# Attention's inner order on one core: one value run at the head of every key step, scores with the second head first, seven and nine products between the runs

## The chip, the cores and the metric

The kernel runs on one core of one Trainium2 chip. The metric is the device time of one execution in microseconds (us), smaller is better. Names of engines as in the profile: PE is TensorE (PEld its weight loads), DVE is VectorE, ACT is ScalarE, POOL is GpSimd, SP is SyncE with its DMA queue.

## The reference

One transformer block on x of shape (1, 2048, 576) with a conditioning vector c: attention with 32 heads of 18 features each, then a gated feed-forward part of width 4608.

```
mod = silu(c) @ w_mod                      # six rows of 576: sa, ca, ga, sb, cb, gb
h   = layernorm(x) * (1 + ca) + sa
q, k, v = heads(h @ wqkv)                  # 32 heads of 18
p   = softmax(q k^T * 18**-0.5)            # over all 2048 keys
x   = x + ga * (p v) @ wo
h   = layernorm(x) * (1 + cb) + sb
x   = x + gb * (sigmoid(h @ w_gate) * (h @ w_up)) @ w_down
```

## The kernel before, in words

The program has three stretches: layer norm and the q, k, v projections (0 to about 269 us of the profiled execution), attention (to about 1621 us), and the feed-forward part (to the end). The change is in attention.

Attention goes through 32 units. A unit is a pair of heads and one half (1024) of the queries; it takes 16 steps, `kt` = 0 to 15, one for each 128 keys. A step makes four score products, `t` in the order tables (line 955): for each head `h` of the pair and each chunk `c` of 512 queries, keys against queries into a 128x512 tile in PSUM (the on-chip memory for sums), which ACT takes through exp into a tile `p` in SBUF (line 959). Keys and queries of head 0 lie in partitions 0 to 55 and those of head 1 in partitions 64 to 119, so the two heads' products use different halves of PE's rows; each product names one half only.

For the softmax's maximum the kernel runs the products of the unit ahead a second time, queries against keys (`maxima`, line 442, `m` in the tables, one for each call of `turn`). They come in rounds of eight, and their head alternates, 0, 1, 0, 1. Of a round's eight, the first (head 0) is taken up by ACT (line 448, tile `rise`), the third (head 0) by DVE in a custom instruction that also reads `rise` (line 450), and the other six by a DVE maximum (line 455). In each pair of steps one round is done, beginning with its second product: in order the heads are 1, 0, 1, 0, 1, 0, 1, 0, and the last is the one for ACT.

Both kinds of product take their PSUM bank from one ring of seven: `bank()` hands out `s0` to `s6` in turn, so the eighth product waits until the first one's bank has been read by ACT or DVE. The transposes and projections below use the same ring.

`values()` (`v`, line 533) adds probabilities times values for one step, the one two steps back (`LAG`): four products in the program, eight instructions in the trace, each on 32 columns of PE and all 128 rows, into the one bank `o`. Called a value run here. A `w` in the table, once in two steps, is the place for all other work that goes between: `taken` and `outputs` (copy of `o` on ACT, line 547, and four transposes, line 557, once a unit), `spread` (one transpose, line 471, once a unit), and the steps of `rows0` and `rows1` in the second half of attention (transposes at lines 639, 656, 785 and the output projection, line 672, 14 or 9 products at a time).

PE's order is written by hand (`manual_schedule`): it does exactly what the tables say. The other engines' orders are set by a scheduler from the same program.

```
STEPS = "vtmmttmvtm", "tmttwmtmm"      # even kt, odd kt
c, h = divmod(len(probs), 2)           # scores: head 0 first
```

An even step has both value runs; an odd step has none. Read as one cycle, six products lie between the first run and the second (`t m m t t m`), and ten between the second and the next first (`t m t m t t w m t m m`).

Of the kernel before, what the change touches and what calls it, by code (L numbers as in the profile page):

```python
# [15 lines left out]
F32 = mybir.dt.float32  # L16
# [7 lines left out]
P = 128  # L24
# [19 lines left out]
NB = F // 256  # L44
LAG = 2

STEPS = "vtmmttmvtm", "tmttwmtmm"
ORDERED = 56


# [1 line left out]
def tile_block(ctx, tc, x_in, wqkv, wo, w_gate, w_up, w_down, c_in, w_mod, out):  # L52
# [25 lines left out]
    def bank():  # L78

        turns["bank"] += 1  # L80
        return ps.tile([P, 512], F32, name=f"s{turns['bank'] % 7}")


    def load_mod(a, b, i):

        cols = slice(2 * D * i, 2 * D * (i + 1))
        for t in range(0, 4, 2):
            rows = slice(t * P, (t + 2) * P)
            nc.sync.dma_start(a[:, t : t + 2, :], w_mod[rows, cols].rearrange("(t p) c -> p t c", p=P))
        nc.sync.dma_start(b[0:64, :], w_mod[DM:D, cols])  # L90
        return [a[:, t, :] for t in range(4)] + [b]
# [307 lines left out]
    def heads(u):  # L399
        return qsets[u % 3], ksets[u if u < 2 else 2 + (u - 2) % 3]  # L400

    def load_heads(u):


        qs, ks = heads(u)
        half, p = divmod(u, H // 2)
        own = slice(half * HW, (half + 1) * HW)
        for h in range(2):
            rows = slice((2 * p + h) * DH, (2 * p + h + 1) * DH)
            two, one = (slice(64 * h + a, 64 * h + b) for a, b in ((0, 2 * DH), (2 * DH, 3 * DH)))  # L410
            nc.sync.dma_start(
                qs[two, :].bitcast(F32), qd[:, rows, own].rearrange("l f n -> f l n").bitcast(F32)
            )
            nc.sync.dma_start(qs[one, :].bitcast(F32), qd[0, rows, own].bitcast(F32))
            wide = S if h or u < 2 else S + 512
            nc.sync.dma_start(
                ks[two, 0:wide].bitcast(F32),
                kd[0, rows, 0:wide].unsqueeze(1).to_broadcast([DH, 2, wide]).bitcast(F32),
            )
            nc.sync.dma_start(ks[one, 0:wide].bitcast(F32), kd[1, rows, 0:wide].bitcast(F32))  # L420
# [65 lines left out]
    def turn():  # L486
        if turns["s"] < turns["to"]:
            turns["s"] += 1
            next(todo, None)
# [26 lines left out]
    ppool = att.enter_context(tc.tile_pool(name="ppool", bufs=LAG + 1))  # L516
# [25 lines left out]
    def taken():  # L542

        if "whole" in state:
            half, p, acc = state.pop("whole")
            oT = epool.tile([P, 512], F32, name="oT")
            nc.scalar.copy(oT, acc)  # L547
            state["end"] = (half, p, oT)

    def outputs():  # L550

        if "end" not in state:
            return
        half, p, oT = state.pop("end")
        tp = bank().rearrange("p (b q) -> p b q", q=P)
        for b in range(4):
            nc.tensor.transpose(tp[:, b, :], oT[:, b * P : (b + 1) * P], ident)  # L557

        tq = tp.rearrange("p b (j e) -> p j b e", e=32)
        rec = epool.tile([P, 4, 4], F32, name="rec")  # L560
        nc.vector.reciprocal(rec, tq[:, :, :, DH])
        if half == 1 and p == H // 2 - 1:
            state["last"] = epool.tile([P, 512], F32, name="oT")[:, 0 : 16 * DH].rearrange("p (t e) -> p t e", t=8)
            for h in range(2):
                nc.vector.tensor_tensor(
                    state["last"][:, :, h * DH : (h + 1) * DH].rearrange("p (c b) e -> p c b e", c=2),
                    tq[:, 2 * h : 2 * h + 2, :, 0:DH],
                    rec[:, 2 * h : 2 * h + 2, :].unsqueeze(3).to_broadcast([P, 2, 4, DH]),
                    op=ALU.mult,
                )  # L570
            return
        nc.scalar.copy(oT, tp.rearrange("p b q -> p (b q)"))
        tq = oT.rearrange("p (b j e) -> p j b e", j=4, e=32)
        for h in range(2):
            f0 = (2 * p + h) * DH
            nc.gpsimd.tensor_tensor(
                Os[half][:, :, f0 : f0 + DH].rearrange("p (c b) e -> p c b e", c=2),
                tq[:, 2 * h : 2 * h + 2, :, 0:DH],
                rec[:, 2 * h : 2 * h + 2, :].unsqueeze(3).to_broadcast([P, 2, 4, DH]),
                op=ALU.mult,  # L580
            )
# [341 lines left out]
    for u in range(UNITS):  # L923
        half, p = divmod(u, H // 2)
        qs, ks = heads(u)
        if 0 < u < UNITS - 2:
            load_heads(u + 2)
        if u == H // 2:
            Os.append(big.tile([P, 8, 640], F32, name="big"))
        for kt in range(NT):  # L930
            step = u * NT + kt
            turns["to"] = 65 + 4 * LEAD + 4 * (step + 1)
            kcols = slice(kt * P, (kt + 1) * P)
            probs = []
            for does in STEPS[kt % 2]:
                if does == "m":
                    turn()
                elif does == "w":
                    if kt == 3:
                        outputs()  # L940
                    taken()
                    if "spread" in state:
                        spread(*state.pop("spread"))
                    if FROM0 <= step < FROM1:
                        next(rows0, None)
                    if step >= FROM1:
                        next(rows1, None)
                elif does == "v":
                    if step >= LAG:
                        values()  # L950
                else:
                    c, h = divmod(len(probs), 2)
                    sT = bank()
                    rows = slice(64 * h, 64 * h + 3 * DH + 2)
                    nc.tensor.matmul(  # L955
                        sT, ks[rows, kcols], qs[rows, c * 512 : (c + 1) * 512], start=True, stop=True
                    )
                    pr = ppool.tile([P, 512], F32, name=f"p{len(probs)}")
                    state["exp"] = nc.scalar.activation(pr, sT, AF.Exp, scale=SCALE)  # L959
                    probs.append(pr)  # L960
            pending.append((half, p, kt, probs))
            if u in (1, 3):
                if kt == 2:
                    a = big.tile([P, 8, 640], F32, name="big")
                    a = a.rearrange("p a b -> p (a b)")[:, 0 : 8 * D].rearrange("p (t c) -> p t c", t=4)
                    b = slots.tile([P, 2560], F32, name="w0")[:, 0 : 2 * D]
                    mods = load_mod(a, b, 1 + u // 2)
                    row = slots.tile([P, 2560], F32, name="w1")[:, 0:544]
                elif kt == 10 and u == 1:
                    modulate(row, mods, HALVES, [(None, None), (mcol2[:, 1, :], 0.0)])  # L970
                elif kt == 10:
                    modulate(row, mods, HALVES, [(mcol2[:, 0, :], 1.0), (gb_b, None)])
            if 4 * NT <= step < FROM0 and step % 2 == 0:
                next(downs, None)
            if step == FROM0:
                for _ in downs:
                    pass
            if step == FROM1 - 1:
                for _ in rows0:
                    pass  # L980
                bgs.close()
                raws = ctx.enter_context(tc.tile_pool(name="raws", bufs=1, side="right"))
            if u == 30 and kt == 7:
                first = [load_block(raws, 0, k, paced) for k in range(2)]
            if u >= 30 and kt == 2:
                load_x(u - 30, f"k{u - 30}")
            if u == UNITS - 1 and kt == 3:
                nc.sync.dma_start(oend[:, :, 0 : D - DL - 2 * DH], Os[1][:, :, DL : D - 2 * DH])
            if u == UNITS - 1 and kt == 9:
                for _ in rows1:  # L990
                    pass
                load_x(2, "w0")
                load_x(3, "w1")
                both = big.tile([P, 2, 5, 512], F32R, name="big")
                for i in range(2):
                    X[5 + i] = both[:, i]
                    load_x(5 + i)
                begun = {"b": 0, "half": 0, "raw": first}
                for k in ORDER[:2]:
                    weights_operand(begun, k, True)  # L1000
# [281 lines left out]
```

## Time and profile before

| | |
|---|---|
| time, median of 3 runs | 2952.17 us (2949.37 to 2953.37) |
| the profiled execution | 2953.87 us, span 2952.1 us, clock 0.993 |
| attention, about | 269 to 1621 us of the span, 256 pairs of steps |
| PE busy there | 1345.09 of 1352.00 us |
| ACT busy there | 1208.67 us |
| DVE busy there | 1143.04 us |

The span is the time from the first to the last instruction; 1.8 us of the profiled execution lie around it. The profiled execution is 1.7 us above the median of the runs. [...]

### The profile page before, as it was taken

To read this page: it belongs to the slowest core of one execution; us is meant where nothing else is said; L and a number is where in the kernel's file an instruction comes from. 1 tells how busy PE (TensorE), PEld (TensorE's weight loads), DVE (VectorE), ACT (ScalarE), POOL (GpSimd) and SP (SyncE) were. 2 spreads that over 40 slices of the span, in tenths; PEclk is the share of its full clock that TensorE was granted. 3 is DMA by queue.
4 is the path that set the end of the run, shared out by engine and by line. 5 is a ranking of instruction groups with operands and counts; after the bars stand their busy time and mean duration, and the time that the engine had idled before them with its cause. 6 is when DMAs were issued, how large, how long until landed. Compare 5 with 4: busy or idle time off the path is not lost.

```text
span 2952.1 us, 46641 instructions
## 1 busy us (share of the span) xinstructions
PE 2890.3 (98%) x17141; PEld 1888.9 (64%) x17141; DVE 2139.3 (72%) x3896; ACT 1614.7 (55%) x3022; POOL 813.7 (28%) x972
## 2 busy tenths in 40 slices
PE   7999999999999999999999999998999999999999
PEld 5756333433344444444443788877888888888888
DVE  7465888888888888998883777766777555555555
ACT  3214889999999888999889323333333111111111
POOL 3102005444303111464103534467544100000000
PEclk9999999999999999999999999999999999999999
DMA  5325213333302111222214766676666845444443
GB/s 178 101 87 185 71 31 131 121 130 126 117 26 80 53 33 44 90 75 70 60 62 161 271 237 235 232 265 237 217 215 217 317 161 178 166 166 170 162 157 136
DMA packets 137261, 425.97 MB, mean 144 GB/s; under 512 B 18884, under 2 KB 56520, under 8 KB 124744
## 3 DMA queue, kind: packets, MB, share of 16 engines
q1 hardware_dynamic: 121272, 342.42, 34.2%
q0 software_dynamic: 15760, 80.56, 7.6%
q8 instruction: 135, 2.21, 0.3%
q14 instruction: 94, 0.77, 0.1%
HBM read 264.45 MB, written 157.95 MB: 143 GB/s over the span
## 4 chain that ended last, share of the span: by engine, by line
PE 90%; ACT 2%; DVE 2%; DMA 2%; POOL 2%; issue 1%; SPq 1%; POOLq 0%; DVEq 0%; ACTq 0%
PE o L533 17%; PE d L1063 14%; PE x L1027 14%; PE s L955 13%; PE s L442 11%; PE bg L1027 5%; PE bu L1027 5%; PE s L294 4%; PE s L330 2%; PE s L672 2%; ACT p L959 1%; PE s L557 1%; ACT oT L547 1%; POOL S L875 0%; DMA B<-hs 0%
## 5 line engine op out<-in xcount | busy, mean ns | idle before, releaser
L959 ACT ACTIVATE p<-s 128x512 f32<-128x512 f32 x2048 | 1068.5, 608 | 142.9 <-PE s L442 91.7
L455 DVE TENSOR_REDUCE mx<-s 128x1 f32<-128x512 f32 x1568 | 1019.6, 686 | 169.7 <-PE s L442 156.2
L442 PE MATMUL s<-k,q 54*128 54x512 f32 x1920 | 649.7, 439 | 2.1 <-ACT p L959 1.6
L955 PE MATMUL s<-q,k 56*128 56x512 f32 x1920 | 578.7, 433 | 2.6
L955 PEld LDWEIGHTS s<-q,k 56*128 56x128 f32 x1920 | 274.8, 186 | 472.8 <-ACT p L959 304.7
L533 PE MATMUL o<-p,vaug 128*32 128x512 f32 x4096 | 555.8, 608 | 0.0
L1063 PE MATMUL d<-wd,hh 128*128 128x288 f32 x2304 | 470.0, 299 | 17.7 <-DVE Oa L1067 17.1
L1063 PEld LDWEIGHTS d<-wd,hh 128*128 128x128 f32 x2304 | 379.5, 191 | 26.9 <-DVE Oa L1067 21.5
L1067 DVE TENSOR_TENSOR Oa<-Oa,d 128x288 f32<-128x288 f32 x576 | 257.7, 452 | 152.6 <-PE d L1063 149.0
L442 PEld LDWEIGHTS s<-k,q 54*128 54x128 f32 x1920 | 308.4, 185 | 69.3 <-ACT p L959 38.5
L1063 PE MATMUL d<-wd,hl 128*128 128x288 f32 x1152 | 344.0, 299 | 0.0
L1027 PE MATMUL x<-k,w 128*128 128x512 f32 x994 | 239.6, 392 | 2.2 <-DVE u L1241 2.2
L1039 ACT ACTIVATE u<-u 128x512 f32<-128x512 f32 x72 | 45.5, 632 | 328.4 <-DVE u L1229 309.7
L1063 PEld LDWEIGHTS d<-wd,hl 128*128 128x128 f32 x1152 | 219.9, 191 | 0.3 <-DVE hl L1043 0.3
L1027 PEld LDWEIGHTS x<-k,w 128*128 128x128 f32 x994 | 184.7, 188 | 39.6 <-DVE u L1241 2.9
L533 PEld LDWEIGHTS o<-p,vaug 128*32 128x32 f32 x4096 | 83.5, 108 | 164.9 <-issue 149.4
L1069 POOL DMA_DIRECT2D out_dram<-Oa x16 | 8.7, 542 | 607.5 <-DVE Oa L1067 607.5
L1036 ACT ACTIVATE sg<-x 128x512 f32<-128x512 f32 x36 | 21.5, 598 | 282.5 <-PE x L1027 282.5
L450 DVE CUSTOM_DVE_ANT_0 rise<-s,rise 128x512 f32<-128x512 f32 x240 | 163.5, 681 | 0.0
L448 ACT ACTIVATE rise<-s 128x512 f32<-128x512 f32 x240 | 151.4, 631 | 0.0
L914 POOL TENSOR_TENSOR w<-S,w 64x256 fp32r<-64x256 f32 x69 | 72.0, 1044 | 214.2 <-ACT w L909 202.5
L1027 PE MATMUL x<-w,w 128*128 128x512 f32 x504 | 121.3, 390 | 0.0
(240 smaller groups left out, 3812.8 us busy)
## 6 DMA issues: line engine op xcount, KB each, us to landing
w<-ws SPq DMA_DIRECT2D x126, 640.0 KB
ws<-w SPq DMA_DIRECT2D x124, 640.0 KB
wd<-wds SPq DMA_DIRECT2D x36, 1152.0 KB
wds<-w POOLq DMA_DIRECT2D x18, 1152.0 KB, 4.5
k<-kd SPq DMA_DIRECT2D x30, 360.0 KB
w<-in_B_w_down_dram POOLq DMA_DIRECT2D x18, 576.0 KB, 5.0
q<-qd SPq DMA_DIRECT2D x64, 144.0 KB
raw<-in_B_w_gate_dram SPq DMA_DIRECT2D x34, 256.0 KB
```

Source lines behind the costliest of these rows:

```text
L294: nc.tensor.matmul(acc, w, hT[:, t, cols], start=n == 0, stop=n == len(ts_) - 1)
L442: nc.tensor.matmul(sp, qs[rows, qt * P : (qt + 1) * P], ks[rows, kc * 512 : (kc + 1) * 512], start=True, stop=True,)
L448: nc.scalar.activation(rise, sp, AF.Relu)
L450: nc.vector.tensor_tensor_reduce(rise, sp, rise, 1.0, -3.0e38, ALU.add, ALU.max, mx[0][:, qt, 0:1])
L455: nc.vector.tensor_reduce(mx[h][:, qt, j : j + 1], sp, axis=AX.X, op=ALU.max)
L533: nc.tensor.matmul(acc[32 * j : 32 * j + 32, :], vaug[:, kt, (2 * p + h) * VW : (2 * p + h) * VW + 32], probs[2 * c + h], start=kt == 0, s ...
L914: eng.tensor_sub(w[rows, :, to, :], src[rows, :, a, :], w[rows, :, a, :].bitcast(F32))
L955: nc.tensor.matmul(sT, ks[rows, kcols], qs[rows, c * 512 : (c + 1) * 512], start=True, stop=True)
L959: state["exp"] = nc.scalar.activation(pr, sT, AF.Exp, scale=SCALE)
L1027: nc.tensor.matmul(acc[v], w[:, v, a, :], X[s][:, b, :], start=first and n == 0, stop=n == 6, skip_group_check=not first,)
L1063: nc.tensor.matmul(acc[:, :HALF], a[:, f, rows], w[:, f, cols], start=n == 0, stop=n == 5)
L1067: nc.vector.tensor_add(Oa[:, t, cols], Oa[:, t, cols], acc[:, :HALF])
```

## The change

Two edits in the loop over steps. The tables put one value run at the head of each step instead of two in the even step, and move one maximum product from the even step to the odd one. And the scores of a step are taken with head 1 first for each chunk; the tiles keep their names, so `values` reads the same ones in the same order.

```
-STEPS = "vtmmttmvtm", "tmttwmtmm"
+STEPS = "vtmmtmtt", "vmtmttwmtmm"
...
-            probs = []
+            probs, at = [None] * 4, 0
...
-                    c, h = divmod(len(probs), 2)
+                    c, h = at // 2, 1 - at % 2
+                    at += 1
...
-                    pr = ppool.tile([P, 512], F32, name=f"p{len(probs)}")
+                    pr = probs[2 * c + h] = ppool.tile([P, 512], F32, name=f"p{2 * c + h}")
...
-                    probs.append(pr)
```

Read as one cycle, seven products now lie between the first run and the second (`t m m t m t t`) and nine between the second and the next first (`m t m t t w m t m m`). The score product moves from line 955 to 956 and its exp from 959 to 960.

PE in an even step, from the first value run's end through the second run, and one product more. L955 (956) is a score, L442 a maximum product, L533 a value product; the tile behind the operation is the bank. Before:

```order
L955 MATMUL s1_14742<-q0_981,k1_2184 128x512
L442 MATMUL s2_14746<-k2_2187,q1_982 128x512
L442 MATMUL s3_14749<-k2_2187,q1_982 128x512
L955 MATMUL s4_14752<-q0_981,k1_2184 128x512
L955 MATMUL s5_14756<-q0_981,k1_2184 128x512
L442 MATMUL s6_14760<-k2_2187,q1_982 128x512
L533 MATMUL o_14737<-p0_14704,vaug_97 32x512
L533 MATMUL o_14737<-p2_14715,vaug_97 32x512
L533 MATMUL o_14737<-p1_14711,vaug_97 32x512
L533 MATMUL o_14737<-p3_14728,vaug_97 32x512
L955 MATMUL s0_14767<-q0_981,k1_2184 128x512
```

The same place now:

```order
L956 MATMUL s1_14742<-q0_981,k1_2184 128x512
L442 MATMUL s2_14746<-k2_2187,q1_982 128x512
L442 MATMUL s3_14749<-k2_2187,q1_982 128x512
L956 MATMUL s4_14752<-q0_981,k1_2184 128x512
L442 MATMUL s5_14756<-k2_2187,q1_982 128x512
L956 MATMUL s6_14759<-q0_981,k1_2184 128x512
L956 MATMUL s0_14763<-q0_981,k1_2184 128x512
L533 MATMUL o_14737<-p0_14711,vaug_97 32x512
L533 MATMUL o_14737<-p2_14728,vaug_97 32x512
L533 MATMUL o_14737<-p1_14704,vaug_97 32x512
L533 MATMUL o_14737<-p3_14715,vaug_97 32x512
L442 MATMUL s1_14771<-k2_2187,q1_982 128x512
```

A score has come ahead of the second value run, and the run is followed by a maximum product instead of a score.

PE behind the second run, in the pair of steps where the four transposes of a unit's output stand at `w`, before:

```order
L955 MATMUL s0_14767<-q0_981,k1_2184 128x512
L442 MATMUL s1_14771<-k2_2187,q1_982 128x512
L955 MATMUL s2_14774<-q0_981,k1_2184 128x512
L442 MATMUL s3_14778<-k2_2187,q1_982 128x512
L955 MATMUL s4_14781<-q0_981,k1_2184 128x512
L955 MATMUL s5_14785<-q0_981,k1_2184 128x512
L557 MATMUL s6_14789<-ident_66,oT_14717 128x128 x4
L442 MATMUL s0_14803<-k2_2187,q1_982 128x512
L955 MATMUL s1_14806<-q0_981,k1_2184 128x512
L442 MATMUL s2_14810<-k2_2187,q1_982 128x512
L442 MATMUL s3_14813<-k2_2187,q1_982 128x512
```

And now:

```order
L442 MATMUL s1_14771<-k2_2187,q1_982 128x512
L956 MATMUL s2_14774<-q0_981,k1_2184 128x512
L442 MATMUL s3_14778<-k2_2187,q1_982 128x512
L956 MATMUL s4_14781<-q0_981,k1_2184 128x512
L956 MATMUL s5_14785<-q0_981,k1_2184 128x512
L557 MATMUL s6_14789<-ident_66,oT_14717 128x128 x4
L442 MATMUL s0_14803<-k2_2187,q1_982 128x512
L956 MATMUL s1_14806<-q0_981,k1_2184 128x512
L442 MATMUL s2_14810<-k2_2187,q1_982 128x512
L442 MATMUL s3_14813<-k2_2187,q1_982 128x512
```

Five products instead of six stand ahead of the other work, and the same four behind it; what differs in these four is the score's head.

ACT's exps of the same even step, in order, before (p0 and p2 are head 0, p1 and p3 head 1):

```order
L959 ACTIVATE p0_14744<-s1_14742 128x512
L959 ACTIVATE p1_14754<-s4_14752 128x512
L959 ACTIVATE p2_14758<-s5_14756 128x512
L959 ACTIVATE p3_14769<-s0_14767 128x512
```

And now:

```order
L960 ACTIVATE p1_14744<-s1_14742 128x512
L960 ACTIVATE p0_14754<-s4_14752 128x512
L960 ACTIVATE p3_14761<-s6_14759 128x512
L960 ACTIVATE p2_14765<-s0_14763 128x512
```

Head 1 now comes first in each chunk, and all four scores of the even step stand ahead of the second run.

## The prediction

> **What bounds the kernel now.** I read first the stretch of attention by engine, then the chain that ended last, then PE's own order of time in one pair of steps. The windows of attention and of the two halves of one plain pair (start, length, then busy us of each engine):
>
> ```profile
> 269.00:1621.00 1352.00, 1345.09 (x8811) 562.29 (x8812) 1143.04 (x2194) 1208.67 (x2384) 404.95 (x585) 0.99 0.26 84
> 571.58:573.48 1.90, 1.90 (x16) 0.65 (x15) 1.31 (x3) 1.90 (x5) 1.71 (x3) 1.00 0.18 39
> 573.48:576.57 3.09, 3.09 (x21) 1.33 (x19) 3.09 (x7) 2.86 (x7) 1.41 (x3) 1.00 0.64 262
> PE 90%; ACT 2%; DVE 2%; DMA 2%; POOL 2%; issue 1%; SPq 1%; POOLq 0%; DVEq 0%; ACTq 0%
> ```
>
> PE never looks idle, but ACT (4.76 of 4.99 us) and DVE (4.40) are nearly as full. Run to run it is 1.90 us over the six products and 3.09 over the ten. PE's order of time in that pair tells what each piece costs (start, length, line, instructions merged):
>
> ```profile
> 572.57 0.50 PE L955 MATMUL s<-q,k 56*128 56x512 f32 x1
> ...
> 573.48 1.06 PE L533 MATMUL o<-p,vaug 128*32 128x512 f32 x8
> 574.47 0.49 PE L955 MATMUL s<-q,k 56*128 56x512 f32 x1
> 574.47 0.72 PE L442 MATMUL s<-k,q 54*128 54x512 f32 x2
> 574.82 0.63 PE L955 MATMUL s<-q,k 56*128 56x512 f32 x3
> 575.28 0.39 PE L442 MATMUL s<-k,q 54*128 54x512 f32 x1
> 575.65 0.49 PE L955 MATMUL s<-q,k 56*128 56x512 f32 x1
> 575.99 0.65 PE L442 MATMUL s<-k,q 54*128 54x512 f32 x2
> 576.57 1.06 PE L533 MATMUL o<-p,vaug 128*32 128x512 f32 x8
> 577.57 0.50 PE L955 MATMUL s<-q,k 56*128 56x512 f32 x1
> 577.90 0.63 PE L955 MATMUL s<-q,k 56*128 56x512 f32 x2
> 578.15 0.40 PE L442 MATMUL s<-k,q 54*128 54x512 f32 x1
> 578.47 0.64 PE L533 MATMUL o<-p,vaug 128*32 128x512 f32 x4
> ```
>
> A score and a maximum product of different heads start together (574.47). So products cost by slots of two, one for each half of PE's rows. I write T for a score, M for a maximum product, R for the one that ACT takes, X for the one that needs R, with the head behind it. From a run's start to the first slot it is 1.00 us (576.57 to 577.57), the first slot takes 0.34 (574.47 to 574.82), a warm one 0.24 (577.90 to 578.15), the last one before a run 0.33 (578.15 to 578.47). Three slots, T0M1 X0T1 T0M1: 1.00 + 0.34 + 0.24 + 0.33 = 1.90. That half is PE alone.
>
> The ten products are five slots and would take 1.00 + 0.34 + 3 x 0.24 + 0.33 = 2.39. They take 3.09, and the rows of the other engines say why:
>
> ```profile
> 573.14 0.69 DVE L455 TENSOR_REDUCE mx<-s 128x1 f32<-128x512 f32 x1 [0.59 <-PE s L442]
> 574.36 2.57 DVE L455 TENSOR_REDUCE mx<-s 128x1 f32<-128x512 f32 x4
> 575.00 2.07 ACT L959 ACTIVATE p<-s 128x512 f32<-128x512 f32 x4 [0.23 <-PE s L442]
> 575.65 0.18 PEld L955 LDWEIGHTS s<-q,k 56*128 56x128 f32 x1 [0.37 <-ACT p L959]
> ```
>
> The eighth product (575.65) waits for the bank of the first: 0.49 in PE, 0.04 to ACT (574.96 to 575.00), 0.60 in exp (2.07 less three at 0.49), 0.04 back, 1.18 in all. Then come 0.34 (575.99), 0.15 for the last product's bank, and 0.43 from a late last product (about 576.14) to the run at 576.57: 1.00 + 1.18 + 0.34 + 0.15 + 0.43 = 3.10. The wait is a latency, not a full engine.
>
> **The change, part by part.**
>
> *Six become seven.* By heads: T1 M1 X0 T0 M1 T1 T0, four of head 1 and three of head 0. Four slots, T1, M1X0, T0M1, T1T0, against three: + 0.24. Where neighbours have one head the second takes the next slot; its weights load while the first streams, as they do now (in the 0.24 spacing). This term falls on PE's own path, which this half is, in all pairs that have maximum products: 255 pairs less the last 11 or so (89 products are done before the loop, 8 in a pair, 2048 in all), 244.
>
> No row shows the price of two neighbours on one head while the other half is empty. Its bounds: 0, if the lone slot hides under the value run, and 0.34, if it costs a first slot again. I take 0.24, the nearest row, because the run starts 0.33 behind the last slot, longer than a warm slot: nothing lies beside it.
>
> A rule of the Trainium skill bears on this (TensorEngine Tiling (Array Packing), Key Properties): to go over to another tiling mode drains PE. The trace agrees with its 0.33. Without that drain the term would be 0 and the change would gain. The same skill (TensorE: Matmul & The Clock Gate, The mechanism) lets a weight load overlap a product only on another row group; by that each slot would be a product's whole 0.49 and this term 0.49. The 0.24 spacing on one half speaks against it.
>
> *Ten become nine.* M0 T1 M1 T0 T1 (w) M0 T0 M1 R0. Now the first is a maximum product, so the eighth, M1, waits for DVE: 0.50 in PE, 0.07 to DVE (a product begun at 572.57 ends at 573.07; its maximum starts at 573.14), 0.69 for one reduce that follows an idle DVE, some 0.05 back: 1.31. The ninth, R0, has its bank by then (the second product's exp, 1.18) and starts beside M1, since the heads differ; then 0.43. Plain half: 1.00 + 1.31 + 0.43 = 2.74 against 3.09, - 0.35. Bounds: 2.39 if no bank were waited for, 3.09 if nothing were gained. Plain pair: + 0.24 - 0.35 = - 0.11.
>
> *The pairs with other work at `w`.* How many there are (instructions; 4 to a piece at 557, 785 and 639 `Oa`, 3 at 639 `big`, 14 or 9 at 672):
>
> ```profile
> L672 PE MATMUL s<-w,t 128*128 128x288 f32 x336 | 53.2, 304 | 0.5 <-POOL t L647 0.3
> L557 PE MATMUL s<-ident,oT 128*128 128x128 f32 x128 | 21.0, 287 | 0.7 <-ACT oT L547 0.7
> L471 PE MATMUL s<-ident,nm 128*16 128x128 f32 x31 | 8.6, 277 | 0.0
> L785 PE MATMUL s<-ident,z 128*128 128x128 f32 x48 | 7.8, 285 | 0.1
> L672 PE MATMUL s<-we,t 128*128 128x288 f32 x32 | 6.8, 293 | 0.0
> L639 PE MATMUL s<-ident,Oa 128*128 128x128 f32 x32 | 5.3, 287 | 0.0
> L639 PE MATMUL s<-ident,big 128*128 128x128 f32 x24 | 4.3, 289 | 0.0
> L656 PE MATMUL s<-ident,t 128*128 128x128 f32 x8 | 2.6, 328 | 0.0
> ```
>
> That is 32 pieces of projection (16 x 14 + 16 x 9 = 368), 32 + 12 + 16 of several transposes, 31 + 8 of one. About 16 pairs hold two. I count 36 pairs with projection or two pieces, 48 with several transposes, 31 with one, and 130 plain. One of each, the work at `w`, the products behind it and the run (the third after its projections):
>
> ```profile
> 570.14 0.66 PE L557 MATMUL s<-ident,oT 128*128 128x128 f32 x4
> 570.73 0.50 PE L442 MATMUL s<-k,q 54*128 54x512 f32 x1
> 571.07 0.58 PE L442 MATMUL s<-k,q 54*128 54x512 f32 x2
> 571.58 0.64 PE L533 MATMUL o<-p,vaug 128*32 128x512 f32 x4
> ...
> 949.07 1.07 PE L533 MATMUL o<-p,vaug 128*32 128x512 f32 x8
> 950.97 0.33 PE L656 MATMUL s<-ident,t 128*128 128x128 f32 x1
> 951.26 0.50 PE L442 MATMUL s<-k,q 54*128 54x512 f32 x1
> 952.41 1.06 PE L533 MATMUL o<-p,vaug 128*32 128x512 f32 x8
> ...
> 958.25 0.50 PE L955 MATMUL s<-q,k 56*128 56x512 f32 x1
> 958.59 0.40 PE L442 MATMUL s<-k,q 54*128 54x512 f32 x2
> 958.92 1.07 PE L533 MATMUL o<-p,vaug 128*32 128x512 f32 x8
> ```
>
> Here the wait for banks hides under the work already, so the gain of 0.35 isn't there. Two costs come. Behind `w` stood M0 T1, M1 R0: two slots. With the second head first it is M0 T0 M1 R0, three of head 0: three slots, 0.34 + 0.24 + 0.33 = 0.91. Against 0.67 behind projections (958.25 to 958.92) that is + 0.24; against 0.85 behind transposes (570.73 to 571.58, with a bank wait in it) + 0.06. Ahead of `w`, the fifth product T1 takes the bank of the fifth of the seven, M1, which DVE frees late: from the seven's start M1 ends at 0.34 + 0.40 = 0.74, DVE starts at 0.81, and three operations, 0.69 + 0.61 + 0.61 (2.57 less 0.69 over three is 0.63, the nearest row), end at 2.72; with 0.05 it is 2.77. T1 could go at 1.14 + 1.00 + 0.34 + 0.24 = 2.72 with its weights in 0.10 earlier (the late slot's 0.34 against 0.24): 0.15 late. Bounds 0 and 0.15, as a late bank costs no more; I take 0.14, near the upper end, as 0.63 would make the bank later still.
>
> With one transpose, the half ends by banks: R0 needs the third product's, 1.31 + 0.61 behind the first, and 1.00 + 1.92 + 0.43 = 3.35 is what such a half takes today (949.07 to 952.41 is 3.34). So 0 there, and + 0.24 for the pair.
>
> *The copy of `o`* (line 547) stands on ACT ahead of the exp of the score behind the run, before and after; the next value run is two slots and more behind it. Nothing. POOL and SP keep their order of work in attention; their 404.95 us there are far from the end.
>
> *The sum.* Plain 130 x - 0.11 = - 14. Several transposes 48 x (0.24 + 0.06 + 0.14) = + 21. One transpose 31 x 0.24 = + 7. Projections 36 x (0.24 + 0.24 + 0.14) = + 22. Total + 36 us. The profiled execution, 2953.87 us, would be 2990; that run is 1.7 us above the median of the runs, so the median goes from 2952.2 to 2988, 1.2% slower. The feed-forward part is PE's as before and moves as a whole.
>
> **Rivals.**
>
> *Seven and nine end the waits for banks* (the other side). If in plain pairs the eighth product didn't wait, they would take 1.90 + 0.24 + 2.39 = 4.53 against 4.99, 130 x - 0.46 = - 60, with + 50 elsewhere: - 10, 2942. For it: the bursts are more even. Against: M0's bank would have to be free 0.82 behind its start, while PE and one reduce alone take 0.50 + 0.69. It decides from a half of 2.46 on. ACT's 2.07 for four, 0.49 each, would still allow it (9 x 0.49 = 4.4).
>
> *The lone product costs nothing*, because it lies under the run: + 36 - 244 x 0.24 = - 23, 2929. Against: 0.33 ahead of each run.
>
> *DVE isn't late ahead of `w`*: 84 x 0.14 = 12 less, and with a plain half 0.03 shorter, 2972.
>
> *Neighbours on one head pay 0.10 for weights that aren't in yet*: 244 x 0.10 more, and 84 x 0.10 behind `w`, 3021. For it: no row shows weights go in for one half while the other half's turn is not yet come. Against: a product on one half now starts no later than its partner even where its neighbour is on the same head.
>
> *Nothing to measure*: plain pairs at - 0.39 would cancel the rest; a half of 2.46.
>
> **How the numbers follow.** My sum 0.60, DVE not late 0.16, the 0.10 for weights 0.08, waits ended 0.07, lone product free 0.03, cancelled 0.06. The likeliest's own range is 2975 to 3002 (the 0.14 between 0.05 and 0.15, the 2.74 within 0.06). With the case of DVE in time the range is 2964 to 3005; the dear weights and the faster cases stay out. Less than 0.2% (6 us) is what a measurement of this kernel can hardly tell from no change: faster 0.10, same 0.06, slower 0.84.
>
> **What would show it.** Run to run over seven products 2.14 us in all stages; over nine, 2.74 in plain pairs, with the eighth product's weights released by DVE's maximum and no longer by ACT; where projections stand, some 0.4 longer than today. PE's idle and DVE's, ACT's busy times hardly change. I'd be wrong if the seven take 1.90 (lone product hidden) or 2.24 (weights), if the plain half of nine comes near 2.4, or if the halves with projections don't grow.

## The result, and the profile after

The changed kernel takes 2980.86 us (median, 2979.79 to 2982.44) against 2952.77 us for the kernel before: ratio 1.0097, 95% interval 1.0079 to 1.0114. It is 28 us slower; the prediction was 2988 us in a range of 2964 to 3005.

The profiled execution's span is 2979.0 us against 2952.1. The windows of the changed kernel: attention, a plain pair of steps (its two halves from value run to value run), the pair with a unit's four transposes, and a half with 14 products of projection (start and end, length, busy us of PE, PEld, DVE, ACT and POOL; then PE's granted clock, the share of the DMA engines' time, GB/s):

```profile
269.00:1647.00 1378.00, 1371.04 (x8812) 563.21 (x8810) 1146.10 (x2196) 1213.94 (x2384) 405.75 (x585) 1.00 0.25 83
588.85:590.98 2.13, 2.13 (x16) 0.87 (x15) 1.61 (x5) 2.02 (x6) 2.13 (x5) 1.00 0.03 8
590.98:593.69 2.71, 2.71 (x19) 0.95 (x18) 2.71 (x6) 2.61 (x7) 2.71 (x5) 1.00 0.00 0
568.40:570.54 2.14, 2.14 (x17) 0.88 (x16) 1.41 (x3) 2.03 (x6) 2.14 (x5) 1.00 0.51 134
570.54:574.05 3.51, 3.51 (x23) 1.54 (x22) 3.41 (x8) 3.41 (x8) 3.51 (x6) 1.00 0.55 175
1109.72:1114.69 4.97, 4.97 (x33) 3.01 (x32) 3.62 (x8) 3.12 (x7) 0.00 (x0) 1.00 0.00 0
```

Attention takes about 1378 us instead of 1352, while DVE and ACT are busy there for 1146 and 1214 us against 1143 and 1209 before. Seven products take 2.13 from run to run where six took 1.90; nine take 2.71 in a plain pair where ten took 3.09. PE's order of time in the plain pair, and then in the half with transposes:

```profile
588.85 1.07 PE L533 MATMUL o<-p,vaug 128*32 128x512 f32 x8
589.85 0.50 PE L956 MATMUL s<-q,k 56*128 56x512 f32 x1
589.85 0.73 PE L442 MATMUL s<-k,q 54*128 54x512 f32 x2
590.19 0.69 PE L956 MATMUL s<-q,k 56*128 56x512 f32 x2
590.42 0.39 PE L442 MATMUL s<-k,q 54*128 54x512 f32 x1
590.66 0.40 PE L956 MATMUL s<-q,k 56*128 56x512 f32 x1
590.98 1.06 PE L533 MATMUL o<-p,vaug 128*32 128x512 f32 x8
591.98 0.50 PE L442 MATMUL s<-k,q 54*128 54x512 f32 x1
...
593.26 0.50 PE L442 MATMUL s<-k,q 54*128 54x512 f32 x2
...
572.56 0.66 PE L557 MATMUL s<-ident,oT 128*128 128x128 f32 x4
573.14 0.50 PE L442 MATMUL s<-k,q 54*128 54x512 f32 x2
573.48 0.40 PE L956 MATMUL s<-q,k 56*128 56x512 f32 x1
573.72 0.40 PE L442 MATMUL s<-k,q 54*128 54x512 f32 x1
574.05 0.64 PE L533 MATMUL o<-p,vaug 128*32 128x512 f32 x4
```

The seven start in four slots, 589.85, 590.19, 590.42 and 590.66, and in the last one score runs alone. Of the nine, the eighth and ninth start together at 593.26, 1.28 behind the first; the next value run follows at 593.69. PE looks busy through this wait only because its rows last 0.39 to 0.50 each, while products on one half follow each other after 0.23 to 0.34 where nothing holds them. Behind the transposes come three slots, 573.14, 573.48 and 573.72, 0.91 to the run, where two stood; and the transposes start 2.02 behind the run (570.54 to 572.56) instead of 1.90. What the weight loads of the nine waited for, and which engine ended the waits of attention's two kinds of product in all:

```profile
592.57 0.18 PEld L956 LDWEIGHTS s<-q,k 56*128 56x128 f32 x1 [0.29 <-DVE mx L455]
...
593.26 0.19 PEld L442 LDWEIGHTS s<-k,q 54*128 54x128 f32 x2 [0.39 <-DVE mx L455]
...
L956 PEld LDWEIGHTS s<-q,k 56*128 56x128 f32 x1920 | 290.1, 185 | 285.9 <-DVE mx L455 168.0 <-ACT p L960 58.7 <-ACT rise L448 32.7
L442 PEld LDWEIGHTS s<-k,q 54*128 54x128 f32 x1920 | 285.1, 185 | 297.3 <-ACT p L960 204.5 <-DVE mx L455 59.5 <-issue 13.3
```

The eighth product (593.26) and the fifth (592.57) both wait for DVE's maximum now. The largest number in the last row, 204.5 us to ACT, is no wait for a bank: it is the 0.84 us that the weight loads pause during a value run, ahead of the first product of the nine, in 239 pairs.

### The profile page after: what moved, and what is told of

Same layout as the page of the kernel before. It is cut to its first block, busy times and chain, and to the rows that moved or that the text cites. A ratio compares the mean times of both kernels' runs of the same rounds, so it can differ in the third digit from the quotient of the medians.

```text
span 2979.0 us, 47067 instructions
## 1 busy us (share of the span) xinstructions
PE 2915.1 (98%) x17141; PEld 1888.0 (63%) x17141; DVE 2142.8 (72%) x3896; ACT 1618.8 (54%) x3022; POOL 814.5 (27%) x972
## 3 DMA queue, kind: packets, MB, share of 16 engines
q8 instruction: 135, 2.21, 0.3%
## 4 chain that ended last, share of the span: by engine, by line
PE 91%; DMA 3%; DVE 2%; POOL 2%; issue 1%; SPq 1%; ACT 1%; POOLq 0%; DVEq 0%; ACTq 0%
PE o L533 17%; PE s L442 14%; PE x L1027 14%; PE d L1063 14%; PE s L956 12%; PE bg L1027 5%; PE bu L1027 5%; PE s L294 4%; PE s L330 2%; PE s L672 2%; DMA B<-hs 1%; PE s L557 1%; POOL S L875 0%; DMA xs<-ho 0%; DMA w<-ws 0%
## 5 line engine op out<-in xcount | busy, mean ns | idle before, releaser
L442 PE MATMUL s<-k,q 54*128 54x512 f32 x1920 | 632.0, 453 | 2.5 <-ACT p L960 2.2
L956 PE MATMUL s<-q,k 56*128 56x512 f32 x1920 | 614.5, 437 | 1.2 <-DMA q<-mrows 1.2
L533 PE MATMUL o<-p,vaug 128*32 128x512 f32 x4096 | 553.3, 607 | 0.7 <-ACT oT L547 0.7
L442 PEld LDWEIGHTS s<-k,q 54*128 54x128 f32 x1920 | 285.1, 185 | 297.3 <-ACT p L960 204.5
L956 PEld LDWEIGHTS s<-q,k 56*128 56x128 f32 x1920 | 290.1, 185 | 285.9 <-DVE mx L455 168.0
L533 PEld LDWEIGHTS o<-p,vaug 128*32 128x32 f32 x4096 | 83.0, 108 | 172.5 <-issue 153.6
```

Source lines behind the costliest of these rows:

```text
L442: nc.tensor.matmul(sp, qs[rows, qt * P : (qt + 1) * P], ks[rows, kc * 512 : (kc + 1) * 512], start=True, stop=True,)
L533: nc.tensor.matmul(acc[32 * j : 32 * j + 32, :], vaug[:, kt, (2 * p + h) * VW : (2 * p + h) * VW + 32], probs[2 * c + h], start=kt == 0, s ...
L956: nc.tensor.matmul(sT, ks[rows, kcols], qs[rows, c * 512 : (c + 1) * 512], start=True, stop=True)
```

## The experiments

Here a half is the stretch from one value run to the next. Theory: products cost PE slots of two, one for each head; a half with more of one head pays that head's count; and with seven banks the eighth product waits out one eviction. Rivals: the order of heads is nothing; or the halves are long because ACT and DVE are full; or evenness alone ends the waits. Four runs changed the order, two the number of banks, and one put the new order only where it should pay. All times are medians, with ratios to the kernel before.

**Half undone: new tables, head 0 first.**

```
-                    c, h = at // 2, 1 - at % 2
+                    c, h = at // 2, at % 2
```

> The new tables with head 0 first in the scores, as before: half of the change undone. Slot theory (two neighbours on one head take two slots; banks come free by latency): the seven still hold four of one head, 2.13 us. Behind the work at w stand M0 T1 M1 R0 again, two slots instead of three, and the fifth of the seven is no longer late: halves with several transposes 3.50 to about 3.34, with 14 products of projection 4.97 to about 4.60. In plain pairs the ninth product now waits for the second one's exp, which starts a slot late: 2.71 to about 2.81. Sum against the changed kernel: 48 x -0.16 + 32 x -0.36 + 127 x +0.10 = -6, 2971 to 2976. Rival (the order of heads is nothing, the cost is the seven and nine): 2981, halves as in the changed kernel.

Measured: 2975.74 us, ratio 1.0079 (1.0065 to 1.0093). Windows of a plain pair, a half with transposes, one with projection:

```profile
635.76:637.90 2.14, 2.14 (x16) 0.83 (x15) 1.90 (x5) 2.02 (x6) 2.14 (x4) 1.00 0.05 11
637.90:640.80 2.90, 2.81 (x19) 1.20 (x18) 2.69 (x7) 2.60 (x7) 2.90 (x6) 1.00 0.00 0
658.50:661.80 3.30, 3.30 (x23) 1.55 (x22) 3.06 (x8) 2.99 (x8) 3.30 (x6) 1.00 0.48 138
1115.02:1119.62 4.60, 4.60 (x32) 2.82 (x32) 3.19 (x8) 3.09 (x8) 0.00 (x0) 1.00 0.00 0
```

With M0 T1 M1 R0 behind the work at `w` the halves are back at 3.30 and 4.60, about as long as before the change (3.33 and 4.61); the seven still take 2.14. This run takes back two costs at once, the third slot behind `w` and the late start ahead of it; the swap below separates them. The plain half is 2.90, longer than the 2.81 expected. The second product, now of the first one's head, starts 0.34 behind it (638.90 to 639.24); the ninth gets that product's bank 1.14 later (640.38), and the run follows 0.42 behind that (640.80). With 0.24 for the first of these steps it would have been 2.80. That the sum came out inside the expected 2971 to 2976 is in part luck: the plain halves lost more than expected, and the halves with other work gained a little more.

**The other half alone: old tables, head 1 first.**

```
-STEPS = "vtmmtmtt", "vmtmttwmtmm"
+STEPS = "vtmmttmvtm", "tmttwmtmm"
```

> The old tables, six and ten, with head 1 first in the scores: the other half of the change alone. Slot theory: the six are now T1 M1 X0 T0 T1 M1, four of head 1 and two of head 0, so four slots instead of three: 2.13 instead of 1.90 with no product added. The ten are six of head 0 and four of head 1; the plain half still ends by banks, about 3.08; halves with other work grow by 0.24 to 0.47. Sum against before about +90, 3040 to 3050. Rival (head order is nothing): 2953, 1.90 and 3.09.

Measured: 3031.57 us, ratio 1.0272 (1.0258 to 1.0286).

```profile
650.94:653.06 2.12, 2.12 (x15) 0.83 (x15) 1.60 (x5) 2.01 (x6) 2.12 (x4) 1.00 0.03 8
653.06:656.16 3.10, 3.10 (x20) 1.35 (x19) 2.88 (x7) 2.62 (x7) 3.10 (x6) 1.00 0.00 0
1150.85:1155.69 4.84, 4.84 (x34) 3.01 (x33) 3.61 (x8) 3.11 (x7) 0.00 (x0) 1.00 0.00 0
```

This is the cleanest of the runs: six products, with scores and maxima in the same places, and 2.12 instead of 1.90, because four of them are of one head. The rival that head order is nothing falls. The sum is 9 us under the expected, in part since halves with other work grow by 0.20 (transposes, 3.33 to 3.53 by the median) to 0.24 (projection, 4.61 to 4.86) and not by 0.24 to 0.47.

**Fifth and sixth of the seven swapped.**

```
-STEPS = "vtmmtmtt", "vmtmttwmtmm"
+STEPS = "vtmmttmt", "vmtmttwmtmm"
```

> The changed kernel with the fifth and sixth of the seven products swapped (t m m t t m t): the fifth bank is then read by ACT and not by DVE as its third operation. Slot theory with DVE late ahead of w: the halves with several transposes and with projections lose the 0.11 by which that work starts late (2.02 to 1.90 behind the run), plain halves stay 2.71: 80 x -0.11 = -9, about 2972. Rival (the late start at w comes of something else): 2981, the work at w starts at 2.02 still.

Measured: 2970.35 us, ratio 1.0062 (1.0049 to 1.0074), 10 us under the changed kernel. Windows of the plain half of nine, the half with transposes and the one with projection, and PE's order in the second:

```profile
627.32:630.03 2.71, 2.71 (x19) 1.13 (x18) 2.71 (x6) 2.62 (x7) 2.71 (x6) 1.00 0.01 3
647.52:650.92 3.40, 3.40 (x22) 1.54 (x22) 3.35 (x8) 3.30 (x8) 3.40 (x6) 1.00 0.51 157
1102.74:1107.58 4.84, 4.84 (x33) 3.01 (x32) 3.62 (x8) 3.12 (x7) 0.00 (x0) 1.00 0.00 2
...
649.43 0.66 PE L557 MATMUL s<-ident,oT 128*128 128x128 f32 x4
650.01 0.50 PE L442 MATMUL s<-k,q 54*128 54x512 f32 x2
```

The transposes start 1.91 behind the run (647.52 to 649.43), not 2.02, and both halves lose 0.11 to 0.13, while the plain half keeps its 2.71. So DVE's late third maximum was a cost of its own ahead of `w`. The other 0.24 of the half with projection (4.84 here against 4.60 with head 0 first) is the third slot behind `w`, and the order of heads decides it.

**Eight and eight, head 0 first.**

```
-STEPS = "vtmmtmtt", "vmtmttwmtmm"
+STEPS = "vtmmttmtm", "vtmttwmtmm"
-                    c, h = at // 2, 1 - at % 2
+                    c, h = at // 2, at % 2
```

> Eight and eight products between the runs, head 0 first (t m m t t m t m and t m t t w m t m m): an even split without a lone product, four slots each. Slot and bank theory: the eighth product of each half waits 1.18 for the first one's bank, so each plain half is 1.00 + 1.18 + 0.43 = 2.6; plain pair 5.2 against 4.99; total some +50 to +57 against before, about 3005. Rival (evenness ends the waits): halves of 1.00 + 0.34 + 0.48 + 0.33 = 2.15, plain pairs 0.69 shorter, about 2890.

Measured: 3025.90 us, ratio 1.0253 (1.0237 to 1.0269). Both halves of a plain pair, and the weight load of each one's eighth product:

```profile
648.82:651.48 2.66, 2.62 (x18) 1.01 (x17) 2.10 (x6) 2.56 (x7) 2.66 (x5) 1.00 0.03 9
651.48:654.14 2.66, 2.62 (x17) 1.02 (x16) 2.50 (x6) 2.07 (x6) 2.36 (x5) 1.00 0.00 0
...
651.06 0.18 PEld L442 LDWEIGHTS s<-k,q 54*128 54x128 f32 x1 [0.48 <-ACT p L960]
...
653.71 0.18 PEld L442 LDWEIGHTS s<-k,q 54*128 54x128 f32 x1 [0.47 <-ACT p L960]
```

No product is left over here, and still each half waits 0.48: the most even split is far from the fastest. It pays the wait for a bank twice in a pair, where six and ten pay it once. It came 21 us above the expected 3005. The eighth product starts 1.24 behind the first (652.47 to 653.71) and not 1.18: 0.06 in two halves of 130 pairs is 16 us of that; the rest stays open.

**A ring of six banks**, first in the kernel before, then in the changed one.

```
-        return ps.tile([P, 512], F32, name=f"s{turns['bank'] % 7}")
+        return ps.tile([P, 512], F32, name=f"s{turns['bank'] % 6}")
```

> The kernel before with a ring of six PSUM banks instead of seven, all else the same. Bank theory (the eighth product waits for the first one's eviction): now the seventh waits. The six products don't notice, 1.90; the ten take about 3.34 instead of 3.09 in plain pairs, and 0.25 to 0.35 more in halves with other work; some +65, about 3015. Rival (the ten are long because ACT and DVE are full, 4.76 and 4.40 of 4.99 us): neither engine gets more work, so within 10 us of 2952.

> The changed kernel with a ring of six banks. Bank theory: the seven products, which wait for no bank with seven banks, now do: the seventh takes the first one's bank, 1.00 + 1.18 + 0.43 = 2.6 instead of 2.13 in all stages; the nine about 3.3 instead of 2.71 in plain pairs. Some +150 to +176 against the changed kernel with seven, about 3140. Rival (full engines): within 10 us of 2981.

Measured: 3006.24 us, ratio 1.0179 (1.0164 to 1.0195), and 3150.09 us, ratio 1.0669 (1.0654 to 1.0684). Plain pairs of the kernel before with six banks, then of the changed one, with the wait of the latter's seventh product:

```profile
639.34:641.24 1.90, 1.90 (x15) 0.65 (x14) 1.28 (x5) 1.62 (x4) 1.90 (x4) 1.00 0.03 9
641.24:644.58 3.34, 3.27 (x20) 1.51 (x18) 3.34 (x7) 3.01 (x7) 3.34 (x6) 1.00 0.00 0
```

```profile
681.43:684.04 2.61, 2.61 (x16) 1.01 (x16) 1.78 (x6) 1.97 (x5) 2.61 (x5) 1.00 0.02 6
684.04:687.34 3.30, 2.88 (x18) 1.02 (x17) 2.83 (x6) 2.66 (x7) 1.60 (x3) 1.00 0.31 131
...
683.61 0.18 PEld L956 LDWEIGHTS s<-q,k 56*128 56x128 f32 x1 [0.42 <-ACT p L960]
```

No engine had more to do. The six products notice nothing (1.90); the seven, which waited for no bank before, go from 2.13 to 2.61, as one of them now waits out an eviction. One bank less costs the old order 53 us and the new one 169; the old one's is under the expected 65 in part since its second halves at `kt` 0 grow from 3.24 to 3.34 only. So the waits come from the time until one bank is free again, and not from full engines.

**The new order only where it should pay**: in 107 pairs without other PE work and without the copy of `o`; the old order in the rest (`FREE` lists the steps of each unit).

```
+            free = kt // 2 * 2 in FREE.get(u, ())
-            for does in STEPS[kt % 2]:
+            for does in (EVEN if free else STEPS)[kt % 2]:
-                    c, h = at // 2, 1 - at % 2
+                    c, h = at // 2, (at + free) % 2
```

> The changed order (seven and nine, head 1 first) in the 107 pairs of steps that have no other PE work at w and no copy of the value sums, and the old order (six and ten, head 0 first) in all others. Theory: these pairs take 2.13 + 2.71 = 4.84 instead of 4.99 to 5.00, the others 1.90 and 3.33, 3.95, 4.61 as before: 107 x -0.155 = -17, some of it lost where the orders meet; 2936 to 2941, faster than both. Rival (the orders disturb each other at the joins, banks and exps being late into the next pair): within 5 us of 2952 or slower.

Measured: 2944.25 us, ratio 0.9970 (0.9959 to 0.9982): faster than both kernels, though the gain of 9 us is little over half of what was expected. A pair in the new order and the pair behind it in the old one, with one transpose:

```profile
585.62:587.75 2.13, 2.13 (x16) 0.83 (x15) 1.71 (x5) 1.83 (x5) 2.13 (x5) 1.00 0.03 8
587.75:590.46 2.71, 2.71 (x18) 0.94 (x17) 2.71 (x6) 2.61 (x7) 2.71 (x6) 1.00 0.00 0
590.46:592.37 1.91, 1.91 (x17) 0.66 (x15) 1.65 (x4) 1.79 (x5) 1.61 (x3) 1.00 0.00 0
592.37:595.70 3.33, 3.33 (x22) 1.42 (x20) 3.33 (x7) 3.06 (x7) 0.29 (x1) 1.00 0.76 313
```

Each keeps its own time (4.84, and 1.91 and 3.33), so the orders don't disturb each other here. What is missing: in the pairs at `kt` 8 the second half is 2.89 by the median, as in the changed kernel, so nothing is gained in 22 of the 107; and at `kt` 4, behind the transposes, the first half is 2.21. From its first value run to its last, attention is 12.7 us shorter; the stretch ahead of it was 3.8 us longer in this profiled execution (first value run at 276.13 against 272.38), a part whose text the edit doesn't touch. In the other kept traces that run starts anywhere from 269.31 to 275.60; whether the 3.8 is chance or a changed schedule isn't shown.

## Why the prediction was right, point by point

The mechanism held in all four classes of pairs, but not in the plain pairs at `kt` 0 and 8, and the sum was 8 us too high. The halves are medians over the pairs of the profiled execution, before to after, in us; predicted and measured are the change of one pair, and the last column is the measured change of all pairs of the class:

| pairs | first half | second half | predicted | measured | sum of the class |
|---|---|---|---|---|---|
| plain (129, with those at `kt` 0 and 8) | 1.90 to 2.13 | 3.09 to 2.71 | - 0.11 | - 0.15 | - 14 |
| several transposes (46) | 1.90 to 2.13 | 3.33 to 3.50 | + 0.44 | + 0.39 | + 17 |
| one transpose (30) | 1.90 to 2.13 | 3.33 to 3.30 | + 0.24 | + 0.20 | + 6 |
| projection or two pieces (36) | 1.90 to 2.13 | 3.95 to 4.31 (9), 4.61 to 4.97 (14) | + 0.62 | + 0.59, less with two pieces | + 17 |

- *Six become seven, + 0.24*: right, 0.23, in all stages. The head order alone gives it too, with six products. The count by head was right, but not which product is left over: the prediction's slots, T1 then M1X0, would leave the first one alone, and in the trace it is the last (590.66).
- *Ten become nine, 2.74*: right, 2.71; the eighth product waits 1.28 for DVE where 1.31 was worked out. In the pairs at `kt` 0 and 8 it is longer, 2.98 and 2.89 by the median (see below the list). That the class sum is the predicted - 14 all the same is luck: these two against the 0.04 more gained in the other plain pairs.
- *Behind `w`, three slots for two, + 0.24 and + 0.06*: right; the rows show 0.91. With head 0 first the third slot is gone.
- *DVE late ahead of `w`, 0.14*: the mechanism right, 0.12 in size (2.02 against 1.90 behind the run). The swap of fifth and sixth takes it back. That case, to which I gave 0.16 that it would not be there, is closed.
- *The sum*: + 36 predicted; the classes give + 26, some 2 us come off in the last pairs, which have no maximum products, and some 2 are added outside attention: + 27 by the profile. The term mis-sized most is the 36 pairs with projection, 22 against 17: where a transpose and a projection stand together, 0.62 was counted, and the four such pairs with 14 products grew by 0.33 each (6.79 to 7.12). The pairs with several transposes come next, 21 against 17.
- *The rivals*: a lone product under the value run, 1.90, didn't happen, nor the dearer weights, 2.24. That evenness would end the waits fell twice: the nine still wait 0.39 for the eighth, and eight and eight wait in both halves.

In the plain pairs at `kt` 0 and 8 the ninth product starts behind the eighth and not beside it. The two rows, `kt` 0 first, are to be read against 593.26, where the two take 0.50 together:

```profile
567.70 0.77 PE L442 MATMUL s<-k,q 54*128 54x512 f32 x2
...
547.58 0.68 PE L442 MATMUL s<-k,q 54*128 54x512 f32 x2
```

At `kt` 0 the copy of `o`, 566.80 to 567.42 on ACT, stands ahead of the exp that frees the ninth one's bank, and the ninth starts 0.28 behind the eighth. The prediction put the copy at nothing, as it looked only at the next value run. At `kt` 8 the ninth is the first product with another unit's queries and keys. Its bank was free by 547.53, but just ahead of it in PE's queue stand waits for the load of these tiles, issued some 20 us before; it starts 0.21 behind the eighth. No run moves those waits, so that cause is likely but not shown.

The rule that a change of tiling mode drains PE (the Trainium skill, TensorEngine Tiling (Array Packing), Key Properties) agrees with the rows: in none of the nine traces does a value run start beside a lone product; here it starts 0.32 behind it (590.66 to 590.98). No run separates a drain from the plain fact that a value run needs all rows.

## What to carry to other kernels

Where PE packs two products on the two halves of its rows, count products by half, and between any two things that need all rows: where no bank is waited for, the larger count is the time (six products took 1.90 as three and three, 2.12 as four and two), so an odd number or a bad order of heads costs a slot each time, however free the other half is. A burst longer than the ring of PSUM banks waited here, once per burst, until the first product's bank was free again (1.18 to 1.28 us from its start). An even split with both bursts longer than the ring paid that twice, and one bank less cost 53 and 169 us, where the best order won 9. An order that wins in plain steps can lose where other work stands between: choose it step by step.

## What the runs showed of the hardware that was not expected

Products on the two halves of PE's rows don't keep to the program's order. In the seven the program has score, maximum, maximum, and the first two are of the same head. The trace has a maximum product at 589.85 with the score and the other 0.34 later, in the slot that follows (0.73 for the two, 0.39 the second). The one that starts with the score must be the third of the program, as of the two only it is on the other half; the trace doesn't name rows, so that is inferred. It cost nothing here: the slots are four either way. The prediction had let it wait for the second. The Trainium skill (TensorE: Matmul & The Clock Gate, The mechanism) has products start strictly in program order; if the inference holds, these rows speak against that for products on different row groups.
